# Five small moves in an attention and two-MoE kernel: a factor of 0.125, two late fills, a later subtraction, a bank, four exponentials

## The chip, the cores and the metric

The kernel runs on one core of one Trainium2 chip. The metric is device time in microseconds (us). Three runs of the kernel before took 1006.06, 1005.95 and 1005.1 us; their median is 1005.95 us. Beside the times there is one profiled execution, which carries a trace of every engine's instructions. The engines are PE (matrix multiplications), DVE (vector), ACT (activation), POOL (general purpose) and SP (which issues most DMAs). Each works through a queue of its own in a fixed order, and waits only where an operand or a buffer is not ready.

## The reference

Block-causal attention over 4 batches of 8 heads (576 positions, 64 features), then two MoE-like layers on its output, all in float32:

```python
scores = (1.0 / np.sqrt(D)) * np.matmul(q, k.transpose(0, 1, 3, 2))      # factor 0.125
scores = np.where(block_i >= block_j, scores, -1000000000.0)             # blocks of 64
scores = scores - np.max(scores, axis=-1, keepdims=True)
attn = np.exp(scores); attn = attn / (np.sum(attn, axis=-1, keepdims=True) + 1e-09)
x = attn @ v                                    # to (2304 tokens, 512)
h = np.maximum(x @ w_in, 0.0); x = h * h @ w_out                         # w_in 512x2048
h = x @ w_in2                                                            # second layer
g = (a0 + a1*h + a2*h**2 + a3*h**3) / (1.0 + |b0|*|h| + |b1|*h**2 + 1e-6)
out = g @ w_out2
```

## The kernel before, in words

The program is written in units and steps, and a scheduler places each instruction in its engine's queue; what the source sets is which step is issued after which. Two matrix forms are used. Heads 0 to 9 are "plain": their products are single float32 matmuls (four passes). All else splits an operand into a rounded high part and the rest as low part, and sums three products.

**Attention** (lines 180 to 500). A *visit* is a head, or half of one: visits 0 to 7 do the first two row groups of heads 0 to 7, visits 8 to 15 their other two, visits 16 to 39 all four of heads 8 to 31. A *slot* is a visit and a row group; slots count through, and the tiles are named by them: `sy12` or `sx14` is the score bank of slot 12 or 14, `tp12` its transposes. For each slot i the source issues the score matmuls (`emit_s`, L335), the row maximum on DVE (`emit_max`, L358, result in `stat`), the exponential on ACT (`emit_exp`, L371), three slots later the transposes (L300) with the ACT copies (L429 for plain heads) and four slots later the products with v (`emit_pv`, L470 and L483). The maximum is negated and goes into the exponential as its bias. For a plain visit the factor 0.125 (`SCALE`) enters in one of two places: visit 0 takes it in the exponential, as its scale, and then multiplies the maxima by 0.125 on DVE (L363); all later plain visits have POOL multiply the queries, ahead of the scores (`prep_qk`, L253, tile `qr`). For plain heads the row sums of two heads are inverted on DVE (L383, L384, tile `sums`), spread on POOL (L387, `rb`), transposed on PE (L477, `rows`) and multiplied in (L478, L479). Beside this DVE, ACT and POOL convert the first layer's weights (L129 to L141: ACT, DVE, DVE, DVE, DVE, ACT, POOL).

For a split head, the queries are split on ACT (L259) and DVE (L263, into `q_two`); the keys on ACT (L260, `kk`) and POOL (L265, the low part, a subtraction in the lower 64 partitions). `q_two` and `k_two` are two pairs of tiles. Each holds a second copy that is filled once, in `make_two` (L231 and L232, four ACT copies in a row, at slot 36). The attention output goes through a ring: POOL rounds it (L492) and subtracts (L493).

**First layer** (`moe_a`, L528 to L580): blocks of rows are interleaved step by step with the attention slots. `bank` (L528) gives a PSUM bank for each group; from block 4 on (after the last slots) every second one is taken from the tag "tp", whose three banks the attention also uses. Blocks of the second half of the weights follow (L780 `hb`, L821 `yb`).

**Second layer** (from L840): for unit u, twelve matmuls into one of four `h` banks (`hc`, L780), then ACT: |h| into `ab` (L878), the denominator (L879), h's linear term (L880); POOL squares (L881); DVE (L882, L883). One unit later: `ab` = Ln (L862), then Exp gives the starting reciprocal r (L863), DVE refines it and forms g (L864 to L866), ACT and POOL split g (L857, L858, tile `gc`), and PE multiplies it with w_out (L898, `yc`). For units 0 and 1, r lies in the SBUF tile `ab` (two buffers); for all others in the `h` bank itself, so that this bank is free only after L866. The line is `mid[u] = (ab, w, t, ab if u < LAG else h)`, with LAG = 2.

Of the kernel before, what the change touches and what calls it, by code (L numbers as in the profile page):

```python
# [11 lines left out]
AF = mybir.ActivationFunctionType  # L12
ALU = mybir.AluOpType
# [4 lines left out]
P = 128  # L18
S = 576
SP = 640  # L20
D = 64
# [23 lines left out]
def f(ap):  # L45
    return ap.bitcast(F32)
# [3 lines left out]
def attention_moe_moe(ctx: ExitStack, tc: tile.TileContext, q, k, v, wi1, wo1, wi2, wo2, a, b, out):  # L50
# [135 lines left out]
    class Visit:  # L186
        def __init__(self, n, hd, at, gis):
            self.n, self.hd, self.plain, self.at, self.gis = n, hd, hd < PLAIN, at, gis

            self.scale = SCALE if n == 0 else 1.0  # L190

            self.q0, self.q1 = (0, 3 * P) if gis == (0, 1) else (3 * P, SP) if gis == (2, 3) else (0, SP)
            self.k1 = SUB if gis == (0, 1) else S
# [31 lines left out]
    def make_two(un):  # L225
        early.release()
        late = tc.alloc_tile_pool(name="late", bufs=1, reuse_waits="tile")
        for n in range(2):
            q_two.append(late.tile([P, SP], F32R, name=f"q_two{n}"))
            k_two.append(late.tile([P, S], F32R, name=f"k_two{n}"))  # L230
            nc.scalar.activation(q_two[n][D:P], un.qr[D:P], AF.Copy)  # L231
            nc.scalar.activation(k_two[n][D:P], un.kr[D:P], AF.Copy)  # L232
        return late

    def load_v(un):
        src = v[un.hd].rearrange("p (c d) -> p c d", d=D)
# [12 lines left out]
    def prep_qk(un, step):  # L249
        if un.plain:  # L250
            if step == 0 and un.scale == 1.0:
                cols = un.qr[:, un.q0:un.q1]
                nc.gpsimd.tensor_scalar(cols, cols, SCALE, 0.0, op0=ALU.mult, op1=ALU.add)  # L253
            return
        if step == 0:
            hd = un.hd
            un.qh = attn.tile([P, SP], F32R, tag="qh", name=f"qh{hd}", bufs=2)
            un.kk = attn.tile([P, S], F32R, tag="kk", name=f"kk{hd}", bufs=2)
            nc.scalar.activation(un.qh, un.qr, AF.Copy, scale=SCALE)  # L259
            nc.scalar.activation(un.kk, un.kr, AF.Copy)  # L260
        else:
            un.q2, un.k2 = q_two[un.hd % 2], k_two[un.hd % 2]
            nc.vector.scalar_tensor_tensor(  # L263
                un.q2[0:D], un.qr[0:D], SCALE, f(un.qh[0:D]), op0=ALU.mult, op1=ALU.subtract)
            nc.gpsimd.tensor_tensor(un.kk[D:P], un.kr[D:P], f(un.kk[D:P]), op=ALU.subtract)  # L265
            nc.sync.dma_start(f(un.k2[0:D]), f(un.kk[0:D]))

    def prep_v(un, step):
# [184 lines left out]
    def emit_pv(un, half):  # L453
# [35 lines left out]
        if odd:  # L489
            at = S * (b_ % 2)  # L490
            xh, xl = (ring[:, z, hp, at + first:at + end] for z in range(2))
            nc.gpsimd.tensor_scalar(xh, xp[:, 0:n], 1.0, 0.0, op0=ALU.mult, op1=ALU.add)  # L492
            nc.gpsimd.tensor_tensor(xl, xp[:, 0:n], f(xh), op=ALU.subtract)  # L493
            nc.sync.dma_start(xs[:, hp, S * b_ + first:S * b_ + end], xp[:, 0:n])

    wA = {}
# [25 lines left out]
    def moe_a(k):  # L522
# [5 lines left out]
        def bank(nm):  # L528
            nonlocal count
            count += 1  # L530
            tag = "tp" if end_ and count % 2 else "mm"
            return ps1.tile([P, 512], F32, tag=tag, name=nm, bufs=BANKS[tag])

        gs = []
# [109 lines left out]
    for i in range(NI + 5):  # L644
# [25 lines left out]
        advance(steps(i + 1) - steps(i + 0.5), gate)  # L670
        if i == 4 * PLAIN - 4:
            late = make_two(slots[i][0])
        for back in range(4):
            n = units_at.get(i - back)
            if n is None:
# [173 lines left out]
    for u in range(max(downs) + 1):  # L849
# [19 lines left out]
        if u < len(units):  # L869
# [11 lines left out]
            squared = (nc.vector if u >= len(units) - END else nc.gpsimd).tensor_tensor(w, w, ab, op=ALU.mult)  # L881
            nc.vector.tensor_tensor(t, h, t, op=ALU.mult)  # L882
            done = (taken, nc.vector.scalar_tensor_tensor(t, t, a1, h, op0=ALU.add, op1=ALU.mult))  # L883
            mid[u] = (ab, w, t, ab if u < LAG else h)
            if j + 1 < len(blocks3) and 3 <= m < 3 + 2 * KK and m % 2:
                with tc.issue_after(taken.ins), tc.issue_after(squared.ins):
                    split_x(xt[j + 1], m // 2 - 1, blocks3[j + 1][1])
# [81 lines left out]
```

## Time and profile before

| | |
|---|---|
| median of three runs | 1005.95 us |
| profiled execution | 1004.93 us |
| span of its instructions | 1003.2 us |
| PE busy | 992.0 us (99%) |
| DVE busy | 724.8 us (72%) |
| ACT busy | 723.8 us (72%) |
| POOL busy | 570.5 us (57%) |

The span runs from the first instruction to the last; 1.7 us of the profiled execution lie around it. A busy time is the sum over an engine's instructions, so what PE lacks to 1003.2 us is the time in which it had nothing ready. An idle gap of PE comes with a releaser: the instruction whose end let it go on.

### The profile page before, as it was taken

The numbers are of one execution on the slowest core, as the hardware profiler recorded it, in microseconds if no ns is written. First come the engines' busy times: TensorE is split into PE (matmuls) and PEld (weight loads), VectorE is DVE, ScalarE is ACT, GpSimd is POOL, SyncE is SP. The second block draws the span as 40 slices with busy tenths as digits, with TensorE's granted clock in tenths as the row PEclk, the third lists the DMA queues.
The fourth block names the chain that finished last, engine by engine and source line by source line (L and its number), as shares of the span: only waits on it lengthen the run. The fifth ranks groups of instructions, "written<-read, shape, count | busy, mean of one in ns | idle before, by whom it ended". The sixth has DMA issues, their size and how long they took to land.

```text
span 1003.2 us, 16323 instructions
## 1 busy us (share of the span) xinstructions
PE 992.0 (99%) x5361; PEld 864.6 (86%) x5361; DVE 724.8 (72%) x1389; ACT 723.8 (72%) x1590; POOL 570.5 (57%) x617
## 2 busy tenths in 40 slices
PE   8999999999999999999999999999999999999998
PEld 6678999888888899999888887888888888899997
DVE  7898687877787478767768766757666666666765
ACT  7888697887886467655455557867777777787885
POOL 5777597886787268421215386854655554555542
PEclk9999999999999999999999999999999999999999
DMA  9864334334332244569654651002001100200000
GB/s 295 267 198 149 114 113 132 89 106 130 105 107 83 97 131 124 207 184 300 230 191 151 231 157 58 1 1 84 1 1 32 42 1 1 74 1 1 32 1 32
DMA packets 63844, 106.67 MB, mean 106 GB/s; under 512 B 17040, under 2 KB 33424, under 8 KB 63760
## 3 DMA queue, kind: packets, MB, share of 16 engines
q1 hardware_dynamic: 63184, 105.05, 33.5%
q8 instruction: 42, 0.69, 0.3%
q10 hardware_dynamic: 576, 0.59, 0.2%
q14 instruction: 42, 0.34, 0.1%
HBM read 79.30 MB, written 23.07 MB: 102 GB/s over the span
## 4 chain that ended last, share of the span: by engine, by line
PE 91%; ACT 3%; DVE 2%; POOL 1%; DMA 1%; issue 1%; POOLq 0%; DVEq 0%; ACTq 0%; SPq 0%
PE yc L898 19%; PE hc L780 19%; PE hb L780 10%; PE yb L821 10%; PE ya L562 10%; PE ha L540 9%; PE tp L300 5%; PE pv L483 4%; PE sx L335 3%; PE sy L335 2%; PE pv L470 1%; DMA qr<-in_q_dram 1%; DMA raw_ai<-in_wi_dram 1%; POOL rb L387 0%; ACT p L371 0%
## 5 line engine op out<-in xcount | busy, mean ns | idle before, releaser
L780 PE MATMUL hc<-ring,w_ci 128*128 128x512 f32 (+1 forms) x960 | 210.2, 368 | 1.0 <-DVE t L866 1.0
L780 PEld LDWEIGHTS hc<-ring,w_ci 128*128 128x128 f32 x960 | 176.2, 188 | 27.0 <-DVE t L866 1.4
L898 PE MATMUL yc<-w_co,gc 128*128 128x512 f32 x792 | 191.7, 390 | 0.0
L898 PEld LDWEIGHTS yc<-w_co,gc 128*128 128x128 f32 x792 | 148.2, 188 | 29.3
L858 POOL TENSOR_TENSOR gc<-t,gc 128x512 fp32r<-128x512 f32 (+1 forms) x70 | 85.1, 1215 | 89.4 <-issue 61.0
L881 POOL TENSOR_TENSOR wq<-wq,ab 128x512 f32<-128x512 f32 (+1 forms) x78 | 92.8, 1190 | 75.0 <-ACT wq L879 74.7
L540 PE MATMUL ha<-ring,w_ai 128*128 128x512 f32 (+3 forms) x576 | 117.5, 348 | 0.5 <-DVE xp L487 0.5
L821 PE MATMUL yb<-gb,w_bo 128*128 128x512 f32 (+1 forms) x480 | 105.3, 367 | 0.0
L780 PE MATMUL hb<-ring,w_bi 128*128 128x512 f32 (+1 forms) x480 | 105.2, 367 | 0.0
L540 PEld LDWEIGHTS ha<-ring,w_ai 128*128 128x128 f32 x576 | 94.1, 189 | 11.3 <-issue 3.0
L715 POOL TENSOR_TENSOR ring<-ring 128x512 fp32r<-128x512 f32 (+1 forms) x40 | 52.4, 1311 | 88.0 <-ACT ring L714 83.2
L882 DVE TENSOR_TENSOR t<-hc,t 128x512 f32<-128x512 f32 (+1 forms) x80 | 50.9, 636 | 67.7 <-ACT t L880 67.7
L821 PEld LDWEIGHTS yb<-gb,w_bo 128*128 128x128 f32 x480 | 87.6, 188 | 11.4
L780 PEld LDWEIGHTS hb<-ring,w_bi 128*128 128x128 f32 x480 | 87.5, 188 | 11.1
L562 PE MATMUL ya<-gring,w_ao 128*128 128x352 f32 (+3 forms) x480 | 88.9, 331 | 0.0
L864 DVE SCALAR_TENSOR_TENSOR wq<-wq,hc 128x512 f32<-128x512 f32 (+1 forms) x78 | 49.3, 632 | 53.0 <-ACT hc L863 35.6
L300 PE MATMUL tp<-ident,p 128*128 128x128 f32 x480 | 82.1, 281 | 1.4 <-DVE stat L394 1.0
L562 PEld LDWEIGHTS ya<-gring,w_ao 128*128 128x128 f32 x480 | 75.9, 188 | 4.0 <-DVE s L578 0.2
L399 POOL TENSOR_SCALAR p<-p,stat 64x64 f32<-64x64 f32 (+4 forms) x110 | 60.3, 552 | 28.9 <-DVE stat L395 14.4
L443 DVE TENSOR_TENSOR pt<-tp,pt 128x128 fp32r<-128x128 f32 (+2 forms) x176 | 63.2, 391 | 18.6 <-ACT pt L441 11.9
L441 ACT ACTIVATE pt<-tp 128x128 fp32r<-128x128 f32 (+2 forms) x176 | 56.7, 365 | 19.3 <-PE tp L300 17.4
L878 ACT ACTIVATE ab<-hc 128x512 f32<-128x512 f32 (+1 forms) x80 | 44.2, 553 | 36.3 <-PE hc L780 36.0
(157 smaller groups left out, 2099.3 us busy)
## 6 DMA issues: line engine op xcount, KB each, us to landing
kr<-in_k_dram SPq DMA_DIRECT2D x32, 288.0 KB, 3.6
raw_ci<-in_wi_dram SPq DMA_DIRECT2D x16, 512.0 KB, 4.4
raw_co<-in_wo_dram SPq DMA_DIRECT2D x16, 512.0 KB, 4.0
qr<-in_q_dram SPq DMA_DIRECT2D x24, 320.0 KB, 3.2
ring<-xs SPq DMA_DIRECT2D x24, 256.0 KB, 4.2
raw_ai<-in_wi_dram SPq DMA_DIRECT2D x8, 512.0 KB, 5.2
raw_ao<-in_wo_dram SPq DMA_DIRECT2D x8, 512.0 KB, 4.6
raw_bi<-in_wi_dram SPq DMA_DIRECT2D x8, 512.0 KB, 3.9
```

Source lines behind the costliest of these rows:

```text
L300: yield nc.tensor.transpose(ps[:, P * n:P * (n + 1)], ptile(un, t)[:, P * c:P * (c + 1)], ident)
L399: nc.gpsimd.tensor_scalar(pv, pv, st[r:P, 6 + n:7 + n], 0.0, op0=ALU.mult, op1=ALU.add)
L441: nc.scalar.activation(high, src, AF.Copy)
L443: nc.vector.tensor_tensor(low, src, f(high), op=ALU.subtract)
L540: nc.tensor.matmul(ps[:, 0:n], w[:, zw, P * kk:P * (kk + 1)], ring[:, zx, kk, x0:x0 + n], start=i == 0, stop=i == 3 * KK - 1)
L562: nc.tensor.matmul(ps[c][:, 0:n], wA["o", m][:, zw, P * c:P * (c + 1)], gs[m][:, zg, 0:n], start=m == 0 and i == 0, stop=m == HALF - 1 and ...
L715: nc.gpsimd.tensor_tensor(lo, f(lo), f(hi), op=ALU.subtract)
L780: nc.tensor.matmul(ps[:, 0:n], w[:, zw, P * kk:P * (kk + 1)], xt[:, zx, kk, 0:n], start=i == 0, stop=i == 3 * KK - 1)
L821: nc.tensor.matmul(acc[j, c][:, 0:n], wB["o", m][:, zw, P * c:P * (c + 1)], g[:, zg, 0:n], start=m == 0 and i == 0, stop=last and i == 2)
L858: (nc.vector if u - 2 >= len(units) - END else nc.gpsimd).tensor_tensor(g[:, 1, 0:n], t, f(g[:, 0, 0:n]), op=ALU.subtract)
L881: squared = (nc.vector if u >= len(units) - END else nc.gpsimd).tensor_tensor(w, w, ab, op=ALU.mult)
L898: last = nc.tensor.matmul(acc[j, c], g[:, zg, P * c:P * (c + 1)], w3["o", m][:, zw, :], start=m == 0 and i == 0, stop=m == NM - 1 and i == 2)
```

## The change

Five edits. First, visits 1 to 7 also take the factor 0.125 in the exponential: POOL no longer scales their queries, and DVE scales their maxima (two instructions for each visit). Second, `make_two` fills only the first pair of `q_two` and `k_two`; the second pair is filled two slots later, after that slot's exponential in the order of issue. Third, the subtraction L265 is issued after the last issued L493. Fourth, the first four groups of block 4 take no bank of the tag "tp". Fifth, units 2 and 3 of the second layer keep r in `ab`, too.

```diff
...
         def __init__(self, n, hd, at, gis):
             self.n, self.hd, self.plain, self.at, self.gis = n, hd, hd < PLAIN, at, gis
 
-            self.scale = SCALE if n == 0 else 1.0
+            self.scale = SCALE if n < 8 else 1.0
 
             self.q0, self.q1 = (0, 3 * P) if gis == (0, 1) else (3 * P, SP) if gis == (2, 3) else (0, SP)
             self.k1 = SUB if gis == (0, 1) else S
...
         for n in range(2):
             q_two.append(late.tile([P, SP], F32R, name=f"q_two{n}"))
             k_two.append(late.tile([P, S], F32R, name=f"k_two{n}"))
-            nc.scalar.activation(q_two[n][D:P], un.qr[D:P], AF.Copy)
-            nc.scalar.activation(k_two[n][D:P], un.kr[D:P], AF.Copy)
+        fill_two(un, 0)
         return late
+
+    def fill_two(un, n):
+        nc.scalar.activation(q_two[n][D:P], un.qr[D:P], AF.Copy)
+        nc.scalar.activation(k_two[n][D:P], un.kr[D:P], AF.Copy)
 
     def load_v(un):
         src = v[un.hd].rearrange("p (c d) -> p c d", d=D)
...
             un.q2, un.k2 = q_two[un.hd % 2], k_two[un.hd % 2]
             nc.vector.scalar_tensor_tensor(
                 un.q2[0:D], un.qr[0:D], SCALE, f(un.qh[0:D]), op0=ALU.mult, op1=ALU.subtract)
-            nc.gpsimd.tensor_tensor(un.kk[D:P], un.kr[D:P], f(un.kk[D:P]), op=ALU.subtract)
+            with tc.issue_after(spread["xl"].ins):
+                nc.gpsimd.tensor_tensor(un.kk[D:P], un.kr[D:P], f(un.kk[D:P]), op=ALU.subtract)
             nc.sync.dma_start(f(un.k2[0:D]), f(un.kk[0:D]))
 
     def prep_v(un, step):
...
             at = S * (b_ % 2)
             xh, xl = (ring[:, z, hp, at + first:at + end] for z in range(2))
             nc.gpsimd.tensor_scalar(xh, xp[:, 0:n], 1.0, 0.0, op0=ALU.mult, op1=ALU.add)
-            nc.gpsimd.tensor_tensor(xl, xp[:, 0:n], f(xh), op=ALU.subtract)
+            spread["xl"] = nc.gpsimd.tensor_tensor(xl, xp[:, 0:n], f(xh), op=ALU.subtract)
             nc.sync.dma_start(xs[:, hp, S * b_ + first:S * b_ + end], xp[:, 0:n])
 
     wA = {}
...
         def bank(nm):
             nonlocal count
             count += 1
-            tag = "tp" if end_ and count % 2 else "mm"
+            tag = "tp" if end_ and count % 2 and (k > 4 or count > 4) else "mm"
             return ps1.tile([P, 512], F32, tag=tag, name=nm, bufs=BANKS[tag])
 
         gs = []
...
         advance(steps(i + 1) - steps(i + 0.5), gate)
         if i == 4 * PLAIN - 4:
             late = make_two(slots[i][0])
+        if i == 4 * PLAIN - 2:
+            with tc.issue_after(gates["exp"].ins):
+                fill_two(slots[i][0], 1)
         for back in range(4):
             n = units_at.get(i - back)
             if n is None:
...
             squared = (nc.vector if u >= len(units) - END else nc.gpsimd).tensor_tensor(w, w, ab, op=ALU.mult)
             nc.vector.tensor_tensor(t, h, t, op=ALU.mult)
             done = (taken, nc.vector.scalar_tensor_tensor(t, t, a1, h, op0=ALU.add, op1=ALU.mult))
-            mid[u] = (ab, w, t, ab if u < LAG else h)
+            mid[u] = (ab, w, t, ab if u < 2 * LAG else h)
             if j + 1 < len(blocks3) and 3 <= m < 3 + 2 * KK and m % 2:
                 with tc.issue_after(taken.ins), tc.issue_after(squared.ins):
                     split_x(xt[j + 1], m // 2 - 1, blocks3[j + 1][1])
```


The scheduler places the instructions anew, so the edits move more than the lines they touch. Line numbers of the kernel after are 4 higher from L235 on, and up to 7 higher at the end. The first place is the program's start, around the sums of heads 4 and 5 (`sums0`; slots 8 to 11), whose inverse POOL waits for. On DVE before:

```order
L137 TENSOR_SCALAR raw_ai3_222<-raw_ai3_222 128x512
L141 SCALAR_TENSOR_TENSOR cv_ai2_352<-cv_ai2_352,raw_ai2_177 128x512
L138 SCALAR_TENSOR_TENSOR raw_ai3_222<-raw_ai3_222 128x512
L383 TENSOR_SCALAR sums0_148<-sums0_148 128x2x3
L358 TENSOR_REDUCE stat4_136<-sy12_432 64x1
L358 TENSOR_REDUCE stat4_136<-sy12_432 128x1
L384 RECIPROCAL sums0_148<-sums0_148 128x2x3
```

and after, in the same stretch (L367 is the scaling of the maxima):

```order
L367 TENSOR_SCALAR stat3_135<-stat3_135 128x1
L140 TENSOR_SCALAR cv_ai2_354<-cv_ai2_354 128x512
L362 TENSOR_REDUCE stat4_136<-sy12_436 128x1
L138 SCALAR_TENSOR_TENSOR raw_ai3_221<-raw_ai3_221 128x512
L141 SCALAR_TENSOR_TENSOR cv_ai2_354<-cv_ai2_354,raw_ai2_177 128x512
L367 TENSOR_SCALAR stat4_136<-stat4_136 128x2
L362 TENSOR_REDUCE stat5_137<-sy13_455 128x1
L362 TENSOR_REDUCE stat6_138<-sx14_472 64x1
L387 TENSOR_SCALAR sums0_148<-sums0_148 128x2x3
L362 TENSOR_REDUCE stat6_138<-sx14_472 128x1
L367 TENSOR_SCALAR stat5_137<-stat5_137 128x1
L388 RECIPROCAL sums0_148<-sums0_148 128x2x3
```

Scalings of the maxima and the maxima of slots 13 and 14 now stand ahead of the inverse (L384, after it L388); counted from the start, twelve scalings do. On PE, in the same part of the program, before:

```order
L335 MATMUL sx14_467<-kr7_326,qr7_325 128x64
L335 MATMUL sx14_467<-kr7_326,qr7_325 128x192
L335 MATMUL sy15_491<-kr7_326,qr7_325 128x320
L300 MATMUL tp9_0_445<-ident_71,p2_1_97 128x128 x3
L300 MATMUL tp10_0_455<-ident_71,p0_2_107 128x128
L300 MATMUL tp10_0_455<-ident_71,p1_2_110 128x128 x2
L300 MATMUL tp11_0_474<-ident_71,p2_2_112 128x128 x3
L335 MATMUL sy16_523<-kr8_371,qr8_370 128x448
L335 MATMUL sx17_539<-kr8_371,qr8_370 128x288 x2
```

and after:

```order
L304 MATMUL tp8_0_414<-ident_71,p0_1_92 128x128
L304 MATMUL tp8_0_414<-ident_71,p1_1_95 128x128 x2
L339 MATMUL sy16_530<-kr8_374,qr8_373 128x448
L304 MATMUL tp9_0_450<-ident_71,p2_1_97 128x128 x3
L304 MATMUL tp10_0_460<-ident_71,p0_2_107 128x128
L304 MATMUL tp10_0_460<-ident_71,p1_2_110 128x128 x2
L304 MATMUL tp11_0_480<-ident_71,p2_2_112 128x128 x3
L339 MATMUL sx17_546<-kr8_374,qr8_373 128x288 x2
```

The scores of slot 16 (`sy16`, the first of visit 8, whose queries POOL still scales) stand ahead of the nine transposes of slots 9 to 11, which they followed.

The second place is POOL at visit 21, in the middle of the attention; `kk21` is its low key part. Before:

```order
L579 TENSOR_TENSOR gring_152<-s2_4_2891,gring_152 128x512
L265 TENSOR_TENSOR kk21_3008<-kr29_2900,kk21_3008 64x576
L399 TENSOR_SCALAR p3_1_99<-p3_1_99,stat6_138 128x448
L399 TENSOR_SCALAR p4_1_101<-p4_1_101,stat7_139 128x576
L274 TENSOR_SCALAR vs20_3090<-vr20_2980 128x5x64
L579 TENSOR_TENSOR ga2_5_2972<-s2_5_2974,ga2_5_2972 128x512
L276 TENSOR_TENSOR vs20_3090<-vr20_2980,vs20_3090 128x5x64
```

and after:

```order
L403 TENSOR_SCALAR p1_1_95<-p1_1_95,stat0_132 128x192
L583 TENSOR_TENSOR ga2_6_3055<-s2_6_3057,ga2_6_3055 128x512
L496 TENSOR_SCALAR ring_66<-xp18_0_2874 128x320
L497 TENSOR_TENSOR ring_66<-xp18_0_2874,ring_66 128x320
L269 TENSOR_TENSOR kk21_3015<-kr29_2907,kk21_3015 64x576
L403 TENSOR_SCALAR p3_1_99<-p3_1_99,stat2_134 128x448
```

The subtraction `kk21` has moved behind the normalisations and the ring's L496 and L497.

The third place is ACT in the second layer, units 2 to 5. Before:

```order
L879 ACTIVATE wq3_7505<-ab3_7504,cab_73 128x512
L862 ACTIVATE ab2_7456<-wq2_7457,cab_73 128x512
L863 ACTIVATE hc0_2_7443<-ab2_7456,cab_73 128x512
L878 ACTIVATE ab4_7550<-hc0_4_7537 128x512
L880 ACTIVATE t4_7552<-hc0_4_7537,coef_72 128x512
L772 ACTIVATE w_co13_7346<-w_co13_7346 128x512
L862 ACTIVATE ab3_7504<-wq3_7505,cab_73 128x512
L879 ACTIVATE wq4_7551<-ab4_7550,cab_73 128x512
L863 ACTIVATE hc0_3_7491<-ab3_7504,cab_73 128x512
L857 ACTIVATE gc2_7527<-t2_7458 128x512
L878 ACTIVATE ab5_7594<-hc0_5_7581 128x512
```

and after:

```order
L886 ACTIVATE wq3_7512<-ab3_7511,cab_73 128x512
L869 ACTIVATE ab2_7463<-wq2_7464,cab_73 128x512
L870 ACTIVATE ab2_7463<-ab2_7463,cab_73 128x512
L869 ACTIVATE ab3_7511<-wq3_7512,cab_73 128x512
L870 ACTIVATE ab3_7511<-ab3_7511,cab_73 128x512
L864 ACTIVATE gc2_7534<-t2_7465 128x512
L885 ACTIVATE ab4_7557<-hc0_4_7544 128x512
L887 ACTIVATE t4_7559<-hc0_4_7544,coef_72 128x512
L779 ACTIVATE w_co13_7353<-w_co13_7353 128x512
L886 ACTIVATE wq4_7558<-ab4_7557,cab_73 128x512
L864 ACTIVATE gc3_7578<-t3_7513 128x512
```

The first read of unit 4's bank (`ab4<-hc0_4`) stands behind the Ln and Exp of unit 3 and behind `gc2`, all of which it preceded; and `gc3` now stands ahead of unit 5's first read.

## Rows read from the trace of the kernel before

**Rows 1.** The page, part 1: busy us, share of the span, instructions

```profile
PE 992.0 (99%) x5361; PEld 864.6 (86%) x5361; DVE 724.8 (72%) x1389; ACT 723.8 (72%) x1590; POOL 570.5 (57%) x617
```

**Rows 2.** What the matmul queue waited for: total us, times, longest

```profile
PE sy L335 <- POOL qr L253: 1.1, 1, 1.1
PE tp L300 <- DVE stat L394: 1.0, 1, 1.0
PE hc L780 <- DVE t L866: 1.0, 1, 1.0
...
PE ha L540 <- DVE xp L487: 0.5, 1, 0.5
```

**Rows 3.** Timeline of PE, 13 to 29 us: start, us, line, out<-in, [idle before <-releaser]

```profile
13.99 0.33 PE L477 MATMUL rows<-ident,rb 128*128 128x128 f32 x1 [0.27 <-POOL rb L387]
...
27.05 1.15 PE L300 MATMUL tp<-ident,p 128*128 128x128 f32 x9
28.04 1.00 PE L335 MATMUL sy<-kr,qr 128*128 128x448 f32 x2
```

**Rows 4.** Two small DVE operations by line: duration ns min/median/max, first and last start

```profile
L383 DVE TENSOR_SCALAR sums<-sums x10: 155/394/1239, 12.2 to 94.3; 128x6 f32<-128x6 f32 x5, 128x4 f32<-128x4 f32 x5
...
L394 DVE TENSOR_SCALAR stat<-stat x88: 133/154/774, 94.9 to 336.2; 128x1 f32<-128x1 f32 x66, 128x2 f32<-128x2 f32 x22
```

**Rows 5.** Timeline of DVE, 20 to 30 us

```profile
24.01 0.18 DVE L384 RECIPROCAL sums<-sums 128x6 f32<-128x6 f32 x1
...
24.95 0.48 DVE L358 TENSOR_REDUCE stat<-sy 128x1 f32<-128x320 f32 x1
```

**Rows 6.** Timeline of POOL, 20 to 32 us

```profile
23.88 0.86 POOL L493 TENSOR_TENSOR ring<-xp,ring 128x320 fp32r<-128x320 f32 x1
24.70 1.48 POOL L387 TENSOR_SCALAR rb<-sums 128x128 f32<-128x128 f32 x3
...
27.38 0.58 POOL L253 TENSOR_SCALAR qr<-qr 128x256 f32<-128x256 f32 x1
```

**Rows 7.** Timeline of PE, 84 to 86 us

```profile
84.68 0.66 PE L300 MATMUL tp<-ident,p 128*128 128x128 f32 x4 [0.30 <-ACT xp L478]
85.64 0.64 PE L335 MATMUL sy<-kr,qr 128*128 128x448 f32 x1 [0.30 <-ACT p L371]
```

**Rows 8.** L265 on POOL by line: ns min/median/max

```profile
L265 POOL TENSOR_TENSOR kk<-kr,kk x22: 1406/1588/2063, 84.5 to 309.6; 64x576 fp32r<-64x576 f32 x22
```

**Rows 9.** Timeline of DVE, 188 to 191 us

```profile
188.56 2.09 DVE L263 SCALAR_TENSOR_TENSOR q_two<-qr,qh 64x640 fp32r<-64x640 f32 x1
```

**Rows 10.** Timeline of DVE, 210 to 212 us

```profile
210.94 0.49 DVE L487 TENSOR_TENSOR xp<-pv,tmp 64x320 f32<-64x320 f32 x1
```

**Rows 11.** Timeline of PE, 214 to 215 us

```profile
214.48 0.41 PE L335 MATMUL sx<-kk,qh 128*128 128x320 f32 x1
```

**Rows 12.** L866 with r in the tile ab: ns min/median/max

```profile
L866 DVE SCALAR_TENSOR_TENSOR t<-t,coef,ab x2: 752/1210/1669, 614.0 to 616.1; 128x512 f32<-128x512 f32 x2
```

**Rows 13.** Timeline of DVE, 616 to 633 us

```profile
616.14 1.67 DVE L866 SCALAR_TENSOR_TENSOR t<-t,coef,ab 128x512 f32<-128x512 f32 x1
...
632.38 0.74 DVE L866 SCALAR_TENSOR_TENSOR t<-t,coef,hc 128x512 f32<-128x512 f32 x1
```

**Rows 14.** Timeline of POOL, 617 to 624 us

```profile
617.22 1.75 POOL L773 TENSOR_TENSOR w_co<-w_co 128x512 fp32r<-128x512 f32 x1
...
622.69 1.30 POOL L881 TENSOR_TENSOR wq<-wq,ab 128x512 f32<-128x512 f32 x1
```

**Rows 15.** Timeline of ACT, 622 to 630 us

```profile
622.75 0.60 ACT L878 ACTIVATE ab<-hc 128x512 f32<-128x512 f32 x1
...
629.11 0.67 ACT L863 ACTIVATE hc<-ab,cab 128x512 f32<-128x512 f32 x1
```

**Rows 16.** Timeline of PE, 633 to 639 us

```profile
633.85 1.98 PE L898 MATMUL yc<-w_co,gc 128*128 128x512 f32 x8
635.66 2.88 PE L780 MATMUL hc<-ring,w_ci 128*128 128x512 f32 x12
```

## Prediction

> **What bounds the kernel now.** I read the page first. PE is busy for 992.0 of the 1003.2 us of the span [rows 1], and no other engine comes near. A faster DVE, ACT or POOL is therefore worth nothing by itself: time can be saved only out of the 11.2 us in which PE had nothing ready, some of which lies at the start and between the ends of pipelined matmuls. So the second view is the list of what the matmul queue waited for [rows 2]. The reader is to see that the largest waits are single events, each with one releaser: 1.1 us for POOL's scaled queries, 1.0 for `stat` on DVE, 1.0 for L866 in the second layer, 0.5 for `xp`. Each edit aims at one of these, or at two of 0.30 us in the stretch where the four fills stand [rows 7]. Third, I read PE's timeline around each event [rows 3, 7, 11, 16], for what stands behind it. Last come the engines that release it [rows 4 to 6, 8 to 10, 12 to 15], because a wait that goes is worth only what the next-late operand leaves of it.
>
> All five edits together can remove 1.1 + 0.27 + 0.60 + 1.0 + 0.5 + 1.0, about 4.5 us, or 0.45%. What they do to the queues is the larger question.
>
> **Factor in the exponential.** Removed are seven POOL scalings, and with them the 1.1 us wait [rows 2]. Added are fourteen DVE scalings of one or two columns. A row of that kind, L394, takes 0.154 us in the median [rows 4], so they are 14 x 0.154 = 2.2 us of work, on an engine that has hardly a pause between 8 and 34 us. What counts is whom they delay. The order shows two places.
>
> First the inverse of the sums (L384) and with it POOL's `rb` and PE's `rows`. The first `rows` waits 0.27 us already [rows 3]. Ahead of it DVE now has L138, two maxima and four scalings more, about 0.6 + 0.6 + 0.6 us; this wait grows to more than 1 us. That would be given back, since the scores after it no longer wait for scaled queries.
>
> It is slot 16 that decides. Visit 8 is still scaled by POOL, and its `qr` stands behind the third `rb`, which waits for the L384 of `sums0`. Before, that L384 ended at 24.19 [rows 5], `rb` ran from 24.70 for 1.48 us, `qr` from 27.38 for 0.58 [rows 6], and slot 16 began at 28.04 [rows 3]. After, twelve scalings (12 x 0.154 = 1.8) and three maxima (one is 0.48 [rows 5]; for the pair of slot 14 I estimate as much again) stand ahead of L384: 2.8 us, less some 0.2 to 0.8 that DVE no longer loses beside POOL (L383 has a median of 0.394 and a shortest of 0.155 [rows 4]). So L384 ends between 26.2 and 26.8. Then come 1.48 + 0.58 on POOL (w_ai2, which stood between them, now follows): 28.3 to 28.9, or some 0.6 less if POOL's rows shorten too. Slot 16 thus begins about when it did, although PE would be there sooner: what the first edit wins up to this point is lost here. And nine transposes that PE had done before slot 16 (27.05 to 28.04, 0.99 us [rows 3]) are still to do. The loss is 0.99 plus 0 to 0.9 us; I take +1.5. Lower end: only the waits go, -1.4. Upper end: three of the seven two-column scalings take 0.774 instead of 0.154 [rows 4], +3.4.
>
> In L394's rows, the shortest is 0.133 and the longest 0.774 us, for work that does not differ in size by more than a column [rows 4]. The Trainium skill, "SBUF — State Buffer", section "Who interferes with whom", says that DVE's copy-like instructions in a two-port mode and GpSimd exclude each other for a whole instruction, and that `tensor_scalar` can enter such a mode. By that rule the two-column scalings wait for whatever POOL is doing; the rows agree as far as their spread shows it, and by it the sum would lie toward the upper end.
>
> **Late fills.** Two of four ACT copies move past slot 38's exponential. Both 0.30 us waits [rows 7] are for ACT work behind the four copies. They go, and the copies come at a place where DVE's second `q_two` part now stands ahead of a first-layer square; PE's next bank there was free only just in time. -0.6 in all; range -0.6 to 0 (all given back).
>
> **The later subtraction.** L265 took 1.41 to 2.06 us [rows 8]. At 188.56 DVE's L263, begun beside it, took 2.09 us [rows 9], and the chain behind it ended in the 1.0 us wait for `stat` [rows 2]. After, L263 runs without it, and 0.9 us goes. The price: L265 now follows the ring's L492 and L493. At visit 21, `xp` is done at 211.43 [rows 10] and the scores begin at 214.48 [rows 11]. Into these 3.05 us must now go L492, L493 (0.86 [rows 6]) and L265 (1.41): 0.78 is left for L492 and whatever POOL has in hand. I put 0.15 us on four of the ten odd visits from 13 to 31, 0.6 in all. Sum -0.3. Lower end -1.0 (no wait returns). Upper end: L265 at 2.06 instead of 1.41 takes the rest of that reserve, 0.35 us at each of ten visits less the 1.0: +2.5.
>
> **The bank.** The 0.5 us wait of block 4's third group for a "tp" bank goes [rows 2]. In its place an attention product stands directly behind the transposes of the last slot and must wait for their copies, which that chain did in the shadow of the first-layer matmuls. -0.2; from -0.5 to +0.5.
>
> **Exponentials of units 2 and 3 in SBUF.** The 1.0 us wait of unit 6 for L866 [rows 2] goes: its bank is free once unit 2's L883 is done. But the refinement of units 2 and 3 now reads two SBUF operands where it read PSUM and SBUF. Units 0 and 1 show the price: L866 took 0.752 and 1.669 us with r in `ab` [rows 12], the second beside a POOL operation from 616.14 to 617.81 [rows 13], and the next POOL operation, issued at 617.22, took 1.75 where another took 1.30 [rows 14]. The two engines go in turn: 0.55 us of DVE after POOL's end, 1.15 of POOL after DVE's.
>
> The Trainium skill, in the same section, says it as a rule: a DVE instruction with two SBUF inputs and a GpSimd instruction that reads SBUF block one another, the later one fully. The trace agrees, by 1.669 against 0.752 us. A sum by the opposite rule, that the place of r costs nothing, stands below as the end at -0.8.
>
> Worked out: POOL holds 622.69 to 623.99 [rows 14], so unit 2's L864 ends at 624.5 instead of 623.5, POOL's next at 625.7, L865 at 626.25, L866 (t2) at 627.0. On ACT, `gc2` waits for it, and `ab4` stands behind `gc2`: it begins at 627.6 instead of 622.75 [rows 15]. Before, ACT needed from there to unit 4's Exp ten steps in 6.36 us [rows 15], 0.64 each with one short wait, 0.605 without; after, it is eleven steps, so Exp starts at 634.3 and ends at 634.9. Then four DVE operations of about 0.68: L866 of unit 4 ends at 637.6 (before: 633.12 [rows 13]). Unit 8 needs that bank. PE began it at 635.66, with four matmuls of unit 3's product still behind it (eight of twelve were done) [rows 16]; they now stand ahead (0.9), and the 1.0 us wait is gone with its restart: PE is there at 635.4. It waits 2.2 us. Net -1.0 + 2.2 = +1.2. Lower end, without blocking: t2 comes 2.0 us sooner, unit 8 waits 0.2, -0.8. Upper end: `gc3` also has to wait for t3, 1.2 us more, +2.4.
>
> **Sum.** +1.5 - 0.6 - 0.3 - 0.2 + 1.2 = +1.6 us. The profiled execution took 1004.93 us, with a span of 1003.2 and 1.7 around it: 1006.5 after. It lies 1.0 us under the median of the runs, 1005.95, so against that median I forecast 1007.5 us. A measurement of this kernel can tell about 0.2%, 2.0 us, from no change. The forecast lies within that, close to its edge.
>
> **Rivals.** *The waits simply go (faster).* If DVE's scalings hide in the time that POOL's seven scalings stop costing it, slot 16 starts 1.0 us sooner; and if unit 2's refinement falls between POOL's operations, unit 8 does not wait. Then -1.0 - 0.6 - 0.5 - 0.3 - 0.8 = -3.2: 1002.8 us. For it: the single waits are real and each edit meets its own. Against it: the inverse is behind twelve more scalings by the order, and POOL was busy without a pause around 622 us.
>
> *They cancel.* The first edit costs less, +0.5 (L384 at 26.2 and short `rb`), unit 8 waits 1.0: 0.5 - 0.6 - 0.3 - 0.2 + 0 = -0.6, 1005.3 us. For it: DVE's losses beside POOL before are spread and not all seen in one view.
>
> *The subtraction delays the scores (slower).* At the odd visits from 13 to 31 PE waits for `kk`. It decides from the point at which L265, L493 and POOL's work in hand together exceed the 3.05 us of visit 21; 0.35 us at ten visits is 3.5 us in place of the 0.6 in the sum: +1.6 + 2.9 = +4.5, 1010.4 us. For it: L265's longest row, 2.06 [rows 8], exceeds the shortest by about the reserve. Against it: it is that long beside L263, from which it is moved.
>
> **How the numbers follow.** Forecast (both order losses as worked out; from 1006.0 to 1009.5) 0.50: of it 0.25 below 1007.95 and 0.25 above. The waits simply go: 0.16, of it 0.13 below 1003.95. They cancel: 0.18, of it 0.16 within 2.0 us and 0.02 faster. The subtraction delays the scores: 0.16, all slower. So faster 0.15, same 0.44, slower 0.41. The range 1003.4 to 1010.4 leaves out about half of the first rival and half of the last, 0.16; the forecast's own is 1006.0 to 1009.5.
>
> **What would show it.** Right: the wait of 1.1 for `qr` of visit 6 is gone, but slot 16 waits 1 to 2 us for its `qr`, with nine transposes behind it; unit 8's first matmul waits about 2 us for L866, L864 or L865 of units 2 and 3 take over 1 us beside POOL; no wait at 84.68, 85.64, 191.58 and at unit 6. Wrong: slot 16 starts at 27 us or sooner; L866 of units 2 and 3 at 0.75 us; waits for `kk` at odd visits over 0.3 us each, or new waits in stretches that none of these steps names.

## The result, and the profile after

The change made the kernel slower: 1015.12 us median against 1006.0 (six runs each; ratio 1.0095, interval 1.0078 to 1.0111). It was forecast to become slower, but the 1007.5 us and the range up to 1010.4 were far too low. The profiled execution has a span of 1012.9 us, 9.7 more than before. PE has as many instructions as before and is busy only 2.9 us longer [rows 1], so most of the time must stand in new waits. (One execution of a later run, with three `ab` buffers, took 4572.82 us at a granted clock of 0.206 and is left out of that run's ratio.)

```profile
PE 994.9 (98%) x5361; PEld 866.3 (86%) x5361; DVE 728.4 (72%) x1403; ACT 723.4 (71%) x1590; POOL 564.5 (56%) x610
```

The next view lists what the matmul queue waited for (total us, times, longest). Of the waits aimed at [rows 2] none is left in its old place, but the list is longer than before:

```profile
PE hc L787 <- DVE t L873: 2.4, 1, 2.4
PE sy L339 <- POOL qr L256: 2.2, 1, 2.2
PE sx L339 <- POOL kk L269: 1.9, 4, 0.5
...
PE ha L544 <- DVE s L582: 1.2, 1, 1.2
PE pv L487 <- ACT pt L445: 1.0, 3, 0.5
...
PE pv L487 <- DVE stat L398: 0.7, 1, 0.7
PE pv L487 <- DVE xp L491: 0.6, 1, 0.6
```

To see which edit costs what, I took the start of the same matmul in both traces (us) and how far it has fallen behind. Heads and visits have to be kept apart here: the 10, 13 or 21 in `kk21` is the head, and by the count of visits given above head 21 is visit 29, with slots 84 to 87. Where the change and the working say "visit 21" or "the odd visits from 13 to 31", heads are meant.

| matmul | before | after | behind |
|---|---|---|---|
| slot 36 (factor done) | 76.92 | 80.60 | 3.7 |
| slot 41 (fills done) | 95.01 | 98.73 | 3.7 |
| slot 52 (head 13) | 128.80 | 133.72 | 4.9 |
| slot 85 (head 21) | 214.48 | 220.45 | 6.0 |
| a late product with v | 341.78 | 349.74 | 8.0 |
| second layer, first unit | 599.93 | 607.96 | 8.0 |
| next block's first unit | 682.81 | 692.23 | 9.4 |

**The factor.** PE from 26 to 34 us [rows 3], then DVE, then POOL [rows 5, 6]:

```profile
26.32 0.55 PE L304 MATMUL tp<-ident,p 128*128 128x128 f32 x3
29.11 1.02 PE L339 MATMUL sy<-kr,qr 128*128 128x448 f32 x2 [2.25 <-POOL qr L256]
29.96 1.95 PE L304 MATMUL tp<-ident,p 128*128 128x128 f32 x9
31.70 2.05 PE L339 MATMUL sx<-kr,qr 128*128 128x288 f32 x4
```

```profile
26.68 0.18 DVE L388 RECIPROCAL sums<-sums 128x6 f32<-128x6 f32 x1
```

```profile
27.03 1.22 POOL L391 TENSOR_SCALAR rb<-sums 128x128 f32<-128x128 f32 x3 [2.19 <-DVE sums L388]
28.22 0.83 POOL L256 TENSOR_SCALAR qr<-qr 128x256 f32<-128x256 f32 x1
```

The chain is the forecast one: the inverse ends at 26.86 instead of 24.19, `rb` and `qr` follow, and slot 16 starts 1.07 us late with nine transposes behind it. These took 1.95 us where they took 1.15 before. The reason stands in the windows of the same stretch (busy time of each engine; the number behind POOL's is the granted clock):

```profile
29.00:30.00 1.00, 0.90 (x3) 0.47 (x4) 0.99 (x2) 1.00 (x5) 1.00 (x2) 1.00 1.06 321
30.00:31.00 1.00, 1.00 (x7) 1.00 (x6) 0.84 (x2) 0.60 (x2) 1.00 (x2) 0.57 0.98 210
31.00:32.00 1.00, 1.00 (x6) 1.00 (x5) 0.31 (x2) 1.00 (x4) 0.92 (x3) 0.50 0.73 139
32.00:33.00 1.00, 1.00 (x3) 0.71 (x3) 0.00 (x0) 0.58 (x3) 1.00 (x4) 0.50 0.83 329
33.00:34.00 1.00, 1.00 (x3) 0.19 (x3) 0.21 (x1) 0.00 (x0) 1.00 (x2) 0.73 0.39 147
```

After the gap PE ran for some 3.4 us (worked out from these rows) at the lower level, 1.2 GHz. In the trace of before, every window from 26 to 35 us has a granted clock of 1.00.

**The subtraction.** POOL, DVE and PE around the scores of head 21 and head 13 [rows 8 to 11]. First POOL, with DVE's L266 beside it:

```profile
216.80 0.82 DVE L266 SCALAR_TENSOR_TENSOR q_two<-qr,qh 64x640 fp32r<-64x640 f32 x1
216.86 1.08 POOL L496 TENSOR_SCALAR ring<-xp 128x320 fp32r<-128x320 f32 x1 [1.11 <-DVE xp L491]
218.03 0.88 POOL L497 TENSOR_TENSOR ring<-xp,ring 128x320 fp32r<-128x320 f32 x1
218.98 1.42 POOL L269 TENSOR_TENSOR kk<-kr,kk 64x576 fp32r<-64x576 f32 x1
```

In the kernel before, L265 stood in that place behind `xp`, with L263 beside it:

```profile
211.46 0.82 DVE L263 SCALAR_TENSOR_TENSOR q_two<-qr,qh 64x640 fp32r<-64x640 f32 x1
211.51 2.06 POOL L265 TENSOR_TENSOR kk<-kr,kk 64x576 fp32r<-64x576 f32 x1 [1.09 <-DVE xp L487]
```

PE in the changed kernel, and DVE in front of PE's first wait:

```profile
133.29 0.33 PE L487 MATMUL pv<-pt,vs 128*128 128x128 f32 x1 [0.71 <-DVE stat L398]
...
220.45 0.41 PE L339 MATMUL sx<-kk,qh 128*128 128x320 f32 x1 [0.51 <-POOL kk L269]
```

```profile
130.86 1.43 POOL L269 TENSOR_TENSOR kk<-kr,kk 64x576 fp32r<-64x576 f32 x1
131.02 1.95 DVE L266 SCALAR_TENSOR_TENSOR q_two<-qr,qh 64x640 fp32r<-64x640 f32 x1
```

At head 21 POOL needs 216.86 to 220.40 for the three, and the scores wait. The same happens at 197.75 (head 19), 286.98 (head 27) and 309.67 (head 29). What these four share is L496: it begins 0.06 us after DVE's L266 (that of the next head) and takes 1.08 us. The eight other L496 of this form from 104 us on have no L266 beside them and take 0.46, and no scores wait for `kk` behind them. Without the 0.62 us more, the three would have fitted. In the kernel before, the instruction beside L263 was L265 itself, with 2.06 us.

The second reading is the reverse case. At 130.86 the moved L269 of head 13 begins 0.16 us before L266 of head 14. This L266 takes 1.95 us where it took 0.81 in that place before, and PE waits 0.71 us for what stands behind it (the view names `stat`). The collision that the edit removes at 188.56 [rows 9] has new places.

**The second layer.** ACT, DVE and PE, up to the first matmul of unit 8 [rows 12 to 16]:

```profile
635.07 0.63 ACT L864 ACTIVATE gc<-t 128x512 fp32r<-128x512 f32 x1 [1.55 <-DVE t L873]
635.61 0.58 ACT L885 ACTIVATE ab<-hc 128x512 f32<-128x512 f32 x1
```

```profile
630.86 1.69 DVE L871 SCALAR_TENSOR_TENSOR wq<-wq,ab 128x512 f32<-128x512 f32 x1 [1.71 <-POOL w_ci L780]
632.59 1.66 DVE L872 SCALAR_TENSOR_TENSOR ab<-wq,ab 128x512 f32<-128x512 f32 x1
```

```profile
645.86 2.33 PE L787 MATMUL hc<-ring,w_ci 128*128 128x512 f32 x9 [2.38 <-DVE t L873]
```

`ab4` is the ACT row at 635.61. Less the 8.0 us by which PE is behind, it starts at 627.6, where the working put it.

### The profile page after: what moved, and what is told of

Same layout as the page of the kernel before. It is cut to its first block, busy times and chain, and to the rows that moved or that the text cites. A ratio compares the mean times of both kernels' runs of the same rounds, so it can differ in the third digit from the quotient of the medians.

```text
span 1012.9 us, 16319 instructions
## 1 busy us (share of the span) xinstructions
PE 994.9 (98%) x5361; PEld 866.3 (86%) x5361; DVE 728.4 (72%) x1403; ACT 723.4 (71%) x1590; POOL 564.5 (56%) x610
## 4 chain that ended last, share of the span: by engine, by line
PE 87%; DVE 5%; ACT 5%; POOL 2%; issue 1%; POOLq 0%; ACTq 0%; DVEq 0%
PE yc L905 18%; PE hc L787 18%; PE hb L787 10%; PE yb L828 10%; PE ya L566 9%; PE ha L544 8%; PE tp L304 4%; PE pv L487 3%; PE sx L339 3%; PE sy L339 2%; PE pv L474 1%; DVE stat L362 1%; POOL kk L269 1%; ACT p L375 1%; DVE pt L447 1%
## 5 line engine op out<-in xcount | busy, mean ns | idle before, releaser
L871 DVE SCALAR_TENSOR_TENSOR wq<-wq,hc 128x512 f32<-128x512 f32 (+1 forms) x76 | 47.9, 631 | 51.5 <-ACT hc L870 35.9
```

## The experiments

Each run was timed beside runs of the kernel before on the same chip; these lie at 1005.4 to 1005.75 us in the median. A ratio is the run's time against theirs, with its 95% interval. "Behind" is again PE's lag against the one trace of before. Two things limit it: the span of that trace, 1003.2 us, is 0.5 below the median span of the kernel before (1003.7 in 97 executions), and the traces of edits 2 and 4, of head 20 and of the three `ab` buffers are 0.5 to 0.7 us behind at 26 us already, before their edit acts.

**Edit 1 alone** (`self.scale = SCALE if n < 8`).

> The first edit alone. Theory (queue and clock): slot 16 waits 2.2 us for its scaled queries with nine transposes still to do, and TensorE's clock then stands at half for 3 to 4 us; +3.7 us against the kernel before, of it some 1.7 us in rows at half clock. Rival (queue only, as forecast): +1.5 us, and the low clock of the trace of after is a chance of that execution.

1007.17 us, ratio 1.0018 (1.0009 to 1.0027), so +1.8 us by the ratio. In the trace PE is 2.2 us behind after slot 18, 2.7 for a while, and 2.2 to 2.4 to the end:

```profile
29.09 1.02 PE L335 MATMUL sy<-kr,qr 128*128 128x448 f32 x2 [2.27 <-POOL qr L253]
29.95 1.15 PE L300 MATMUL tp<-ident,p 128*128 128x128 f32 x9
30.93 1.14 PE L335 MATMUL sx<-kr,qr 128*128 128x288 f32 x4
```

The same gap, at full clock: nine transposes take 1.15 us. So the queue is worth 2.2 to 2.3 in the trace, and the clock's share in the whole (0.80 on the transposes, 0.91 on the next scores) does not follow from the gap alone. The theory, with the clock, was wrong here. The rival's +1.5 lies within the interval of the times (0.9 to 2.7 us), but is 0.7 below the trace.

**Edit 1 with the gap filled**, ten matmuls of ones into a "mm" bank ahead of slot 16:

```diff
+        if i == 16:
+            fill = ps1.tile([P, 512], F32, tag="mm", name="fill16", bufs=2)
+            with tc.issue_after(marks[-1].ins):
+                for _ in range(10):
+                    filled = nc.tensor.matmul(fill[:, 0:P], ones[:, 0:P], ones[:, P:2 * P], start=True, stop=True)
```

> The first edit alone, with ten matmuls on constants (their result is never read) placed on PE right ahead of slot 16, in the time in which it waits for the queries. Theory (clock): the wait is filled, the clock stays at 2.4 GHz, and 1.5 to 2.0 us of the first edit's loss are gone: +1.7 us against the kernel before. Rival (the loss is the wait alone): no better than the first edit alone, +3.7 us.

1011.17 us, 1.0046 (1.0033 to 1.0059). Its time tells nothing on slot 16, and neither expectation fits: a wait of 2.6 us (`hb` for an ACT copy) came at 407.7 us, with half clock until 417, and PE falls 5.7 us further behind there. (That the extra tile shifts which bank each later group takes is the likely reason; no run shows it.) The trace up to 400 us does tell something. The clock is full from 27 to 35 us, and PE is 2.2 us behind, as in edit 1 alone. That run was at full clock, too, so there was no clock loss to save.

**The factor in the exponential for visit 8 too** (`n < 9`), so that slot 16 waits for no queries.

> As the first edit, but visit 8 takes the factor in the exponential as well, so that slot 16 needs nothing from POOL. Theory (slot 16 waits for POOL's scaled queries, behind the sums' inverse): the 2.2 us wait at 27 to 29 us is gone, the loss of the first edit, +2.2 us, shrinks to +1 us or less. Rival (the scalings on DVE delay exponentials and copies as such): two more scalings, the loss stays at +2.2 us or grows, as waits for copies or exponentials.

1007.3 us, 1.0018 (1.0009 to 1.0026). PE is 2.5 behind from slot 18 on. The wait of 2.2 us at slot 16 is gone and one comes later:

```profile
31.04 0.55 PE L300 MATMUL tp<-ident,p 128*128 128x128 f32 x3 [1.53 <-DVE xp L479]
```

It is for another operand that comes through the same late DVE, whose inverse ends at 26.99 here. The loss did not shrink, against the theory: the queue of `qr` was only where it surfaced.

**Edit 1 with the scalings on POOL:**

```diff
-            nc.vector.tensor_scalar(st[:, 0:n], st[:, 0:n], SCALE, None, op0=ALU.mult)
+            (nc.vector if un.n == 0 else nc.gpsimd).tensor_scalar(st[:, 0:n], st[:, 0:n], SCALE, 0.0, op0=ALU.mult, op1=ALU.add)
```

> Edit 1 alone, but the maxima of visits 1 to 7 are scaled by POOL instead of DVE (visit 0 stays on DVE). Theory (edit 1's loss is the fourteen scalings ahead of the inverse of the sums in DVE's order): without them DVE keeps its old order, L384 of the second sums0 ends near 24.2 us as before, slot 16 waits under 1 us, and the loss at slot 18 is under 1.0 us instead of 2.3; time within 1 us of the kernel before. Rival (fourteen small operations cost the exponentials the same wherever they stand, since each maximum now passes through one more engine): the loss at slot 18 stays 1.5 to 3 us, with waits of the transposes for p, spread over slots 2 to 15.

1005.29 us, 0.9995 (0.9986 to 1.0004), as the theory has it. DVE's inverse and slot 16:

```profile
24.30 0.19 DVE L384 RECIPROCAL sums<-sums 128x6 f32<-128x6 f32 x1
```

```profile
26.38 1.02 PE L335 MATMUL sy<-kr,qr 128*128 128x448 f32 x2 [0.26 <-POOL qr L253]
```

The inverse is back where it was, and PE is 0.2 to 0.3 ahead from slot 18 to slot 40 and level after, instead of 2.2 to 2.4 behind. The loss of edit 1 is DVE's queue.

**Edit 2 alone** (the second pair filled two slots later).

> The second edit alone. Theory (given back at once: the first-layer group that follows slot 40's scores waits for DVE's square, whose bank had been free just in time): within 0.3 us of the kernel before in the trace, the two waits of 0.30 us gone, a new one of about 1.2 us behind slot 40's scores. Rival (as forecast): -0.6 us, and the new wait belongs to the third edit.

1004.99 us, 0.9997 (0.9988 to 1.0006), which can't be told from no change. In the trace PE gains 0.4 by slot 41 and 0.65 by the end, with a new wait of 0.49 at 91.41 (`ha` for `s` of DVE). The wait of the theory is there, but not the 1.2 us of it. In the whole it grows to 1.16 and takes all.

**Edit 3 alone** (L265 after the last L493).

> The third edit alone (L265 behind the ring's subtraction). Theory (the scores wait for kk, and products for copies that moved): +4 us, with waits of 0.4 to 0.5 us for kk at visits 19, 21, 27, 29 and no wait of 1.0 us for stat. Rival (the forecast's -0.3: the mid-kernel loss of after comes from the shifted phase that the first edit leaves): within 1 us of the kernel before.

1010.51 us, 1.0048 (1.0036 to 1.006), so +4.8 us. The list of waits shows the new ones of the whole again:

```profile
PE sx L336 <- POOL kk L266: 1.9, 4, 0.5
...
PE pv L484 <- ACT pt L442: 1.0, 3, 0.5
...
PE pv L484 <- DVE stat L395: 0.7, 1, 0.7
```

PE goes from level at slot 36 to 0.6 us behind at slot 45 and 4.8 at the end. From slot 45 on that is 4.1, as in the whole (4.3). The first 0.6 comes where the fills save theirs, so part of what the fills lose in the whole is this edit's; the two can be counted there as 0 and +4.3 or as -0.4 and +4.8, and the runs do not separate them.

**Edit 3 for even heads** (`if un.hd % 2 == 0`).

> The third edit for even heads only (their scores begin 4 to 8 us after the moved L265 could end); odd heads keep L265 where it was. Theory (the odd visits' scores wait for kk, and that is most of the loss): none of the four kk waits, each 0.65 us with its restart, and the 1.0 us wait for stat gone too; between -1 and +1 us. Rival (any move of L265 past the ring's work delays normalisations, transposes' copies and products): still +2 us or more, without kk waits.

1006.27 us, 1.0011 (1.0002 to 1.002). No wait for `kk`, none of 0.7 for `stat`. PE loses 0.6 by slot 45, gains 0.8 at slot 77 and loses 0.7 by slot 105, 0.5 in all against 4.8; the time, +1.1, lies at the upper end of the theory. So the 4 us belong to the odd heads.

**Edit 3 for head 20 alone**, where L263 took 2.09 us.

> Edit 3 for head 20 alone, the visit at which L263 took 2.09 us beside L265 and the 1.0 us wait for stat stood. Theory (the saving of edit 3 is this one place, the cost is everything else): the wait of 1.0 us at 191.6 goes and no wait for kk comes; -0.6 to -1.1 us, ratio 0.9988 to 0.9996. Rival (each moved subtraction costs some 0.3 us behind the normalisations, that of head 20 too): the same time as before within 0.4 us.

1005.75 us, 1.0001 (0.9993 to 1.001). The trace shows the saving:

```profile
189.34 0.82 DVE L263 SCALAR_TENSOR_TENSOR q_two<-qr,qh 64x640 fp32r<-64x640 f32 x1
```

PE gains 0.8 at slot 77 (0.78 behind, then level). In the time it is not seen: this trace is 0.5 behind by slot 12, ahead of the edit's place. By time the run is inconclusive.

**Edit 4 alone** (no "tp" bank for four groups).

> The fourth edit alone. Theory (one wait for another): the 0.5 us wait of block 4 for xp is gone, an attention product waits 0.5 to 0.6 us for a copy of the last transposes; 0.0 us, within 0.2. Rival (as forecast): -0.2 us.

1005.72 us, 1.0004 (0.9995 to 1.0013). The 0.5 us wait for `xp` goes, and a product waits 0.6 for `xp` instead, as the theory has it; PE loses 0.2 there.

**Edit 5 alone** (`ab if u < 2 * LAG`).

> The fifth edit alone (units 2 and 3 keep r in SBUF). Theory (order and blocking as worked out): unit 8 waits 2.2 to 2.4 us, unit 6 no longer 1.0; +1.4 us. Rival (no blocking): unit 8 waits at most 0.2 us; -0.8 us.

1008.25 us, 1.0026 (1.0017 to 1.0035), so +2.6 us where the theory had +1.4. Unit 6 does not wait, unit 8 waits 2.38. The profiled execution had two stretches of half clock, at 23 to 27 us after a gap of 1.08 (the kernel before has the same gap, 1.07, and full clock behind it), and after unit 8's:

```profile
22.00:23.00 1.00, 0.07 (x1) 0.07 (x1) 1.00 (x2) 1.00 (x5) 1.00 (x2) 1.00 1.05 381
23.00:25.00 2.00, 2.00 (x8) 1.91 (x9) 1.44 (x6) 1.41 (x5) 2.00 (x3) 0.52 1.13 336
...
642.00:644.00 2.00, 2.00 (x6) 1.51 (x6) 1.03 (x2) 2.00 (x4) 1.70 (x2) 0.50 0.00 0
```

Of the eleven executions, the three at a mean granted clock of 0.999 or 1.000 have spans of 1004.2 to 1005.2 us, the eight at 0.996 to 0.998 have 1006.1 to 1008.6. The first lie 0.5 to 1.5 over the median span before, which fits the +1.4; the rest goes with the clock.

**Edit 5 with three `ab` buffers** (`"ab": 3`), which lets `ab4` stand early again.

> The kernel before with edit 5 (units 2 and 3 keep r in ab) and three ab buffers instead of two. With them the first reads of units 4 and 6 stand early in ACT's order again, ahead of the split parts that they followed in edit 5 alone; the refinement of units 2 and 3 still has two SBUF operands. Theory (edit 5's loss is the buffer: ab4 waits for unit 2's refinement, and unit 4's bank comes free late): unit 8 waits at most 0.5 us, unit 6 not at all, PE about 1 us ahead of the kernel before after unit 8: -1.0 us, ratio 0.9985 to 0.9997. Rival (the loss is the blocking between DVE's refinement and POOL): unit 8 still waits 1.5 us or more, the time stays +1 to +2.5 us over the kernel before.

1006.87 us, 1.0009 (1.0 to 1.0018). A second run gives the trace:

> Edit 5 with three ab buffers once more, for its trace. Theory (buffer): unit 6 does not wait and unit 8 waits at most 0.5 us; where the time of the timed runs (+0.9 us over the kernel before) goes must then show elsewhere. Rival (blocking): unit 8 waits 1.5 us or more.

```profile
630.40 2.88 PE L898 MATMUL yc<-w_co,gc 128*128 128x512 f32 x12
634.26 3.01 PE L898 MATMUL yc<-w_co,gc 128*128 128x512 f32 x12 [0.98 <-ACT gc L857]
637.12 2.88 PE L780 MATMUL hc<-ring,w_ci 128*128 128x512 f32 x12
```

Units 6 and 8 do not wait, as the buffer theory has it; but PE waits 0.98 for `gc3`, for DVE's two refining steps of unit 3 still take 1.66 us each beside POOL, and 0.24 for a later `gc`. PE loses 0.9 here instead of 1.4, although unit 6's wait is saved in both. So neither expectation fits: the buffer is a part, and the larger part remains without it. That all of this remainder is the blocking is argued from the rows, not shown by a run.

**The change with the scalings on POOL.**

> The changed kernel, all five edits, with the maxima of visits 1 to 7 scaled by POOL instead of DVE. Theory (the factor's loss in the changed kernel is the queue of DVE's scalings, 2.25 us at slot 16, and the half clock that followed that gap, 1.5 us; both go with the scalings): slot 16 waits under 1 us, no half clock between 30 and 34 us, the loss at slot 20 is under 0.5 instead of 3.7 us, and the whole is 3 to 4 us faster than the changed kernel: 1011 to 1012.5 us. Rival (the half clock comes by its own chance or from another place, and the queue alone is worth 2.3): 1012.5 to 1013.5 us, with a half clock somewhere in the first 100 us.

1011.06 us, 1.0055 (1.0042 to 1.0067): 4.1 below the changed kernel, as the theory has it. Slot 16 waits 0.25 us, no half clock follows, and PE is 0.3 behind at slot 36 instead of 3.7. In the profiled execution half clock follows unit 8's gap of 2.35 us instead.

**The change once more.**

> The changed kernel once more, unaltered, for its clock. Theory (the half clock at 30.3 to 33.7 us follows the 2.25 us gap at slot 16 in some executions and not in others): the same waits within 0.2 us, but the half clock may stand at another of the gaps over 1 us, at slot 16 or at unit 8; PE's offsets differ by 1.5 to 1.9 us for each. Rival (it belongs to this kernel's slot 16): half clock at the same place.

1015.48 us. The same gap of 2.25 us at slot 16, but full clock behind it; the half clock stands behind unit 8's gap of 2.38 us this time, where the first trace has full clock:

```profile
32.00:33.00 1.00, 1.00 (x5) 0.30 (x4) 0.69 (x2) 0.79 (x4) 1.00 (x3) 1.00 0.79 266
...
646.00:648.00 2.00, 2.00 (x6) 1.61 (x5) 1.86 (x3) 1.79 (x4) 2.00 (x2) 0.50 0.03 8
```

**What gained, together**: edit 2, edit 3 for head 20, edit 1 with the scalings on POOL.

> The kernel before with three parts that gained or cost nothing in their runs: edit 2, edit 3 for head 20 alone, and edit 1 with the scalings on POOL. Theory (the savings stand in different stretches and add up): -0.65 (fills) -0.9 (head 20) -0.3 (factor) = about -1.8 us, ratio 0.9975 to 0.9990. Rival (each saving is given back at a later wait, as part of them was in their own runs): within 0.5 us of the kernel before.

1004.08 us, 0.9988 (0.9979 to 0.9997): the only version whose interval lies below the kernel before, by a hair. PE is 0.1 ahead at slot 36, 0.5 at slot 45, 1.15 from slot 85 to the end, of the 1.8 that the theory adds up.

By the ratios the five edits alone add up to +0.93% (1.8 - 0.3 + 4.8 + 0.4 + 2.6 = 9.3 us); the whole is +0.95%.

## Why the prediction was wrong

**The step that failed is the later subtraction**: forecast -0.3, measured +4.3 in the whole (alone +4.8 in time and trace), beyond its upper end of +2.5. Two readings failed in it.

First, "I put 0.15 us on four of the ten odd visits". Four heads do wait, but 0.45 to 0.51 us each, which puts PE 0.6 behind at each. At head 21 the reserve was read rightly (3.05 us), and L269 took 1.42 and L497 0.88, as worked out. But L496 took 1.08, not the usual 0.46, where 0.78 was left for it and all else; starts and gaps between the three take 0.3 more. The working knew the collision: L265's 2.06 us stood beside L263, "from which it is moved". It did not ask what takes the place behind `xp`, beside L266. L496 does.

Second, "L263 runs without it" was asked at 188.56 only. The moved instructions pass all heads, and at 130.86 the L269 of head 13 stands ahead of L266 of head 14: 0.71 us of wait, 1.2 behind. (L266 also took 1.57 and 1.56 us at 240.39 and 262.24; PE's lag moves by less than 0.1 there.) The rest stands around two products that wait for ACT's copies, 0.48 at 185.42 and 0.24 at 274.67; PE falls about 0.6 behind around each. The saving is there: 0.8 in the traces, forecast 0.9. The third rival had the mechanism, the place, and a sign of being wrong that came, waits for `kk` over 0.3 us. In place of its 0.35 us at ten heads, 3.5 in all, came 0.6 at four, 2.4 in all, and it left out the collision of head 13.

**The factor** was right in mechanism and place; its size was low, +1.5 against 2.2 to 2.3 in the traces (+1.8 by the time of edit 1 alone, which does not exclude 1.5). Slot 16 came at 29.11 where 28.3 to 28.9 was worked out: the inverse was 0.06 later than the later bound, `qr` took 0.83 instead of 0.58, and the starts between the steps, which had no term, take about 0.2; `rb` was shorter, 1.22 instead of 1.48. The long two-column scalings of the upper end did not come: the eight of L367 took 0.171 us in the mean and 0.250 at most. It is their place ahead of the inverse that costs.

**The clock** had no term. Without half clock the changed kernel has a span of 1011.2 us (the one execution of the six with a mean granted clock of 1.000), 8.0 over the profiled span before and 7.5 over the median span before; the other five, at 0.996 to 0.998, have 1012.0 to 1015.8. The terms measured in the traces, 2.3 + 0 + 4.3 + 0 + 1.4, give the same 8.0. So 7.5 to 8 of the 9.1 us are queues, and the rest goes with the clock.

**The fills** gained 0.4 to 0.65 in their own trace, against 0.6, but nothing in the whole, the upper end given. **The bank** came to 0 in the whole (+0.2 alone in the trace) instead of -0.2. **Units 2 and 3** were right to 0.2: net +1.4 in the trace against +1.2, unit 8 waits 2.38 against 2.2, by the order and the blocking as worked out. The rule of the Trainium skill weighed there ("SBUF — State Buffer", "Who interferes with whom") is borne out: beside POOL L871 and L872 take 1.69 and 1.66 us, and 0.68 and 0.69 at 634.95 and 635.67, where POOL starts nothing until 635.78.

## What to carry to other kernels

A tight engine's small instructions cost by what stands behind them, not by their duration: fourteen of about 0.16 us on DVE cost PE 2.2 to 2.3, and nothing on POOL, which the same edit had relieved. When an instruction is moved at every visit, work out its collisions at every visit that it reaches, not only at the one it is moved for, and ask which instruction takes the place that it leaves; moving it at the one visit kept the gain in the trace. A reserve read from a trace must hold each operation at the length that it has beside its new neighbours.

## What the runs showed of the hardware

The granted clock fell to half, 1.2 GHz, for some 3.4 us (once for nearly 7) behind some gaps of PE and not behind others of the same length, in the same program too: behind 2.25 us (the changed kernel, slot 16), 2.35 to 2.38 (unit 8, in three executions), 2.6 and even 1.08 us; not behind 2.25 (slot 16, the changed kernel once more), 2.38 (unit 8, its first trace), 2.27 (edit 1 alone) and 1.07 (the kernel before). A stretch of 3.4 us cost PE 1.3 to 1.6 us. What decides it the runs do not show.

Where a DVE instruction on two SBUF operands (L266) and a POOL instruction met, the one that began later took longer by most of what was left of the other: L496, begun 0.76 us before L266's end, took 0.62 us more than alone; L266, begun 1.27 us before L269's end, 1.14 more.
